# Attention output tiles moved from a stage of their own into the FFN blocks of a transformer layer, with smaller edge blocks and fewer small instructions

## The chip, the cores and the metric

The kernel runs on one core of a Trainium2 chip. The metric is device time in microseconds (us): the median of several executions. The profile is of one execution; its span is some 1 to 2 us shorter than the time. Engines: PE = TensorE, PEld = its weight loads, DVE = VectorE, ACT = ScalarE, POOL = GpSimd, SP = SyncE.

## The reference

One layer on 2048 tokens of width 576: layernorm with modulation, attention with a softmax feature map (32 heads of 18), output projection with a gate, layernorm again, an FFN of width 4608 with ReLU, and a second gate. Cut to what matters:

```python
pq = einsum('bhsd,hdf->bhsf', q, w_phi); pk = ...          # per head 18x18
phi_q = concat([softmax(pq), softmax(-pq)]); phi_k = ...
kv  = einsum('bhsf,bhsd->bhfd', phi_k, v);  z = phi_k.sum(over tokens)
num = einsum('bhqf,bhfd->bhqd', phi_q, kv)
o   = num / (einsum('bhqf,bhf->bhq', phi_q, z) + 1e-06)
x   = x + ga * (o @ wo)
h   = layernorm(x) * (1 + cb) + sb
x   = x + gb * (relu(h @ w1) @ w2)
```

`kv` sums over all tokens. So no token's attention output can begin before the whole K/V loop is through. After that point every tile of 128 tokens is independent.

## The kernel before

The program has a head (load, fold `w_phi` into Wk and Wq), a K/V loop over 16 token tiles, and then attention output and FFN. The parts that the change touches:

```python
def num_tile(t):                       # 128 tokens: 10 matmuls into three PSUM banks
    ...
    # eight small ACT copies bring the denominators from PSUM to dz
    # DVE: product, sum, reciprocal, product  (4 small instructions)
    # DVE: 4 multiplications PSUM x factor -> tmp
    nc.gpsimd.tensor_tensor(out=o_sb[:, t % NO, :], in0=tm[:, 0, :], in1=tm[:, 1, :], op=ALU.add)

def wo_tile(t):                        # 6 transposes of o_sb, ACT copy to oT, 10 matmuls with wo,
    ...                                # DVE adds the product to x_sb

def attn_out(b):                       # TPB = 4 tiles
    for t in range(b * TPB, (b + 1) * TPB):
        num_tile(t); wo_tile(t)
        ln_stats(1, t); ln_rstd(1, t, t + 1); ln_apply(1, t)
    ...
    to_features(b * TPB, TPB, ps1, h2T[b], 0, mod2, "vavav")     # transposes for the FFN

# ---- order of the program after the K/V loop
attn_out(0)
for b in range(1, NB): q_block(b, q_one)
...                                     # load of the last quarter of w2
for b in range(1, NB): attn_out(b)
for b in range(NB):    ffn1(b, ...); ffn2(b)
```

`ffn1` runs 18 pairs of hidden blocks (per pair eight 128-row and two 64-row matmuls of 512 columns). `ffn2` runs 36 matmuls of 288 columns for each half of each tile. The order on each engine is chosen by the compiler's scheduler from this program order. PE then ran its list in order: in the trace below it stands idle for one tile (1.20 us, to 235.53 us) although FFN matmuls follow in its list.

The softmax here doesn't subtract the row's maximum and nothing guards it: scores larger than these inputs give would overflow.

Of the kernel before, what the change touches and what calls it, by code (L numbers as in the profile page):

```python
# [8 lines left out]
P = 128  # L9
# [26 lines left out]
def kernel(  # L36
# [73 lines left out]
    NX = 4  # L110
    xn = small([P, NX, 640], BF16, "xn")
# [4 lines left out]
    dz = small([P, 2, 2, 2, 32], FP32, "dz")  # L116
    ab = small([P, 2, 5, 64], FP32, "ab")
# [19 lines left out]
    nc.sync.dma_start(x_sb[:, 1, :], xf[:, 1, :])  # L137
# [4 lines left out]
    nc.sync.dma_start(x_sb[:, 2:4, :], xf[:, 2:4, :])  # L142
    load_rows(nc.sync, wmod_sb[0], w_mod[:, 0:D], False)
    load_rows(nc.sync, wmod_sb[1], w_mod[:, D:2 * D], False)
    load_rows(nc.sync, wv_sb, A_wqkv[:, 2 * D:3 * D], True)
    nc.sync.dma_start(x_sb[:, 4:8, :], xf[:, 4:8, :])
    load_rows(nc.sync, wq_raw, A_wqkv[:, 0:D], False)
    nc.sync.dma_start(x_sb[:, 8:16, :], xf[:, 8:16, :])
    load_rows(nc.sync, wmod_sb[2], w_mod[:, 2 * D:3 * D], False)
    for i in (3, 4, 5):  # L150
        load_rows(nc.sync, wmod_sb[i], w_mod[:, i * D:(i + 1) * D], False)
    load_rows(nc.sync, wo_sb, A_wo, True)

    nc.vector.memset(eps_t[:], EPS)
    make_identity(nc, ident[:])
# [45 lines left out]

    def mod_row(i, dst):
        ps = two()
        for hf in range(2):
            for ck in range(NC):
                k = KR[ck]
                nc.tensor.matmul(ps[:, hf, 0:HD2], lhsT=rep[0:k, ck, :],
                                 rhs=wmod_sb[i][0:k, ck, hf * HD2:(hf + 1) * HD2],
                                 start=(ck == 0), stop=(ck == NC - 1))
        nc.scalar.activation(out=dst[:].rearrange("p (b f) -> p b f", b=2), in_=ps[:, :, 0:HD2], func=ACT.Copy)  # L210
# [9 lines left out]
    def fold_transposes(raw, dstT, engs):  # L220
        for g, (h0, nh) in enumerate(GRP):
            f0, nf = h0 * DH, nh * DH
            pt = one().bitcast(BF16)
# [36 lines left out]
    def ln_apply(n, t):  # L260
        y = xn[:, t % NX, :]
        for a, b, src in ((0, 576, 0), (576, 640, 512)):
            nc.vector.tensor_scalar(out=y[:, a:b], in0=x_sb[:, t, src:src + b - a],  # L263
                                    scalar1=rs[:, n, t, 0:1], scalar2=rs[:, n, t, 1:2],
                                    op0=ALU.mult, op1=ALU.add)

    def to_features(t0, nt, psum, dst, col0, mod, engs):
        for n, cs in enumerate(((0, 1), (2, 3), (4,))):
            pt = psum().bitcast(BF16).rearrange("p (c f) -> p c f", c=2)
            for k, ci in enumerate(cs):  # L270
                for j in range(nt):
                    nc.tensor.transpose(pt[:, k, j * P:(j + 1) * P],  # L272
                                        xn[:, (t0 + j) % NX, ci * P:(ci + 1) * P], ident[:, :])
            for k, ci in enumerate(cs):
                o_ = dst[:, ci, col0:col0 + nt * P]
                i_ = pt[:, k, 0:nt * P]
                if engs[ci] == "a":
                    nc.scalar.activation(out=o_, in_=i_, func=ACT.Identity,  # L278
                                         scale=mod[:, 1, ci:ci + 1], bias=mod[:, 0, ci:ci + 1])
                else:  # L280
                    nc.vector.tensor_scalar(out=o_, in0=i_, scalar1=mod[:, 1, ci:ci + 1],
                                            scalar2=mod[:, 0, ci:ci + 1], op0=ALU.mult, op1=ALU.add)
# [63 lines left out]
    def q_block(b, psum):  # L346
        sl = slice(b * TB, (b + 1) * TB)
        for gs in ((0, 1), (2, 3), (4,)):
            pss = psum(len(gs))
            for n, g in enumerate(gs):  # L350
                f0, nf = GRP[g][0] * DH, GRP[g][1] * DH
                for ci in range(4):
                    nc.tensor.matmul(pss[n][0:nf, :], lhsT=wq_sb[:, ci, f0:f0 + nf], rhs=hT[:, ci, sl],
                                     start=(ci == 0), stop=False)
            for n, g in enumerate(gs):
                f0, nf = GRP[g][0] * DH, GRP[g][1] * DH
                b0 = 64 * n
                nc.tensor.matmul(pss[n][0:nf, :], lhsT=wq_sb[b0:b0 + 64, 4, f0:f0 + nf],
                                 rhs=hT[b0:b0 + 64, 4, sl], start=False, stop=True)
            for n, g in enumerate(gs):  # L360
                nf = GRP[g][1] * DH
                for sgn in range(2):
                    nc.scalar.activation(out=Eq[b][0:nf, g, sgn, :], in_=pss[n][0:nf, :], func=ACT.Exp,
                                         scale=1.0 - 2.0 * sgn)
# [6 lines left out]
    fold_transposes(wk_raw, wkT, "a")  # L371
    for t in range(4):
        ln_stats(0, t)
        if t == 0:
            ln_rstd(0, 0, 1)
            ln_apply(0, 0)
    ln_rstd(0, 1, 4)
    for t in range(1, 4):
        ln_apply(0, t)
    mod_columns((0, 1), mod1)  # L380
    fold(wkT, wk_sb, "a")

    ENG_A = "avava"
    to_features(0, 4, one, hT, 0, mod1, "vvava")
    for t in range(NT + 2):
        if t < NT:
            if t % 4 == 0 and t + 4 < NT:
                for u in range(t + 4, t + 8):
                    ln_stats(0, u)
                ln_rstd(0, t + 4, t + 8)  # L390
            k_tile(t)
            v_tile(t)
        if 1 <= t <= NT:
            k_softmax(t - 1)
        if t >= 2:
            kv_tile(t - 2)
        if t < NT:
            if t + 4 < NT or t % 4 != 3:
                pass
            if t % 4 == 2 and t + 2 < NT:  # L400
                for u in range(t + 2, t + 6):
                    ln_apply(0, u)
                to_features(t + 2, 4, one, hT, (t + 2) * P, mod1, ENG_A)
        if t == 1:
            fold_transposes(wq_raw, wqT, "a")
        if t == 3:
            fold(wqT, wq_sb, "a")
        if t == 5:
            nc.gpsimd.tensor_copy(rep[:], siluc[:].unsqueeze(2).to_broadcast([P, NC, P]))
            mod_row(2, ga_row)  # L410
            for ci in range(NC):
                nc.gpsimd.tensor_tensor(out=wo_sb[:, ci, :], in0=wo_sb[:, ci, :], in1=ga_row[:], op=ALU.mult)
        if t == 7:
            mod_row(5, gb_row)
            mod_columns((3, 4), mod2)
        if t == 9:
            q_block(0, q_two)
    for g in range(NG):
        kv_final(g)
    actx.close()  # L420
# [13 lines left out]
    pa = ctx.enter_context(tc.tile_pool(name="pa", bufs=4, space=PS, reuse_waits="tile"))  # L434
    pf = ctx.enter_context(tc.tile_pool(name="pf", bufs=4, space=PS, reuse_waits="tile"))

    def ps1():
        return pa.tile([P, 512], FP32, name="psa")
# [7 lines left out]
    def num_tile(t):  # L446
        b, tok = t // TPB, slice((t % TPB) * P, (t % TPB + 1) * P)
        p0, p1_, p2_ = ps1(), ps1(), ps1()

        def mm(ps, col, g, sgn):  # L450
            nf, w = GRP[g][1] * DH, GRP[g][1] * (DH + 2)
            nc.tensor.matmul(ps[:, col:col + w], lhsT=Eq[b][0:nf, g, sgn, tok], rhs=kvzd[0:nf, g, sgn, 0:w],
                             start=True, stop=True)
        for g in range(3):
            mm(p0, g * 140, g, 0)
        for g in range(3):
            mm(p1_, g * 140, g, 1)
        for sgn in range(2):
            mm(p2_, sgn * 140, 3, sgn)
        for sgn in range(2):  # L460
            mm(p2_, 280 + sgn * 80, 4, sgn)
        d = dz[:, t % 2]
        for sgn, pp in ((0, p0), (1, p1_)):
            v = pp[:, 0:420].rearrange("p (g w) -> p g w", g=3)[:, :, 126:140]
            for k in range(2):
                nc.scalar.activation(out=d[:, k, sgn, 0:21].rearrange("p (g h) -> p g h", g=3),
                                     in_=v[:, :, 7 * k:7 * k + 7], func=ACT.Copy)
        v3 = p2_[:, 0:280].rearrange("p (s w) -> p s w", s=2)
        v4 = p2_[:, 280:440].rearrange("p (s w) -> p s w", s=2)
        for k in range(2):  # L470
            nc.scalar.activation(out=d[:, k, :, 21:28], in_=v3[:, :, 126 + 7 * k:133 + 7 * k], func=ACT.Copy)
            nc.scalar.activation(out=d[:, k, :, 28:32], in_=v4[:, :, 72 + 4 * k:76 + 4 * k], func=ACT.Copy)
        a = ab[:, t % 2].rearrange("p k (s h) -> p k s h", s=2)
        nc.vector.tensor_tensor(out=a[:, 0], in0=d[:, 0], in1=rev_pair(d[:, 1]), op=ALU.mult)
        nc.vector.tensor_tensor(out=a[:, 1, 0], in0=a[:, 0, 0], in1=a[:, 0, 1], op=ALU.add)
        nc.vector.reciprocal(out=a[:, 1, 1], in_=a[:, 1, 0])
        nc.vector.tensor_tensor(out=a[:, 2], in0=rev_pair(d[:, 1]),
                                in1=a[:, 1, 1].unsqueeze(1).to_broadcast([P, 2, H]), op=ALU.mult)
        A = a[:, 2]
        tm = tmp[:, t % NTMP]  # L480
        for sgn, pp in ((0, p0), (1, p1_)):
            nc.vector.tensor_tensor(  # L482
                out=tm[:, sgn, 0:378].rearrange("p (g h e) -> p g h e", g=3, e=DH),
                in0=pp[:, 0:420].rearrange("p (g w) -> p g w", g=3)[:, :, 0:126].rearrange("p g (h e) -> p g h e", e=DH),
# [112 lines left out]
```

## Time and profile before

511.6 us (median of 5; 510.88 to 512.5), span 509.8 us.

| Stage | us | what PE does |
|---|---|---|
| head | 0 to 25 | waits for loads and PSUM copies |
| K/V loop | 25 to 109 | almost full |
| opening: attention output before any FFN matmul | 109 to 156 | starves; from 136.7 us at half clock (0.50) |
| attention tiles mixed with FFN block 0 | 156 to 282 | waits about 1.2 us per tile |
| FFN blocks 1 to 3 alone | 282 to 505 | full |

From the page of the kernel before: the busy shares, then the 40 slices of the span. Each digit is a tenth; PEclk is the granted TensorE clock.

```profile
PE 460.6 (90%) x3259; PEld 275.7 (54%) x3278; DVE 227.0 (45%) x547; ACT 164.1 (32%) x433; POOL 59.6 (12%) x67
PE   1898899999648989898988999999999999999996
PEclk9999989999857999999999999999999999999999
```

PE is the engine that counts. Digits 6 and 4 in the eleventh and twelfth slice (127 to 153 us) and the 8, 5, 7 of the clock below them mark the opening. From 285 us to the last FFN matmul PE has no idle time left to gain: it is busy 219.96 of 220.60 us. In the head the clock row rests on no record: the first one is at 30.9 us. Four transposes take 0.69 us at 6.53 us, and 0.40 us at 235.53 us.

PE's waits of the kernel before in the window from 104 to 162 us, then from 162 to 285 us. The columns are: who waited, for whom, total us, times, longest.

```profile
PE psa L498 <- POOL o_sb L492: 10.9, 4, 5.6
...
PE psa L498 <- POOL o_sb L492: 13.1, 11, 1.5
```

L498 is the transpose of `o_sb`, the first PE work after the chain num, dz, DVE, POOL. It is by far the largest of PE's waits in these 180 us; the next are 1.9 us on `xn` and 1.6 us on `oT`. (Names such as rH, rV and rEQ in the lines are regions of memory that several tiles share.)

The timeline of PE in that opening (start, us, what, and in brackets the idle time before it and who ended it):

```profile
128.38 1.14 PE L287 MATMUL psa<-wo_sb,oT 128*128 128x288 bf16 x8
132.16 0.40 PE L358 MATMUL psf<-rH 64*72 64x512 bf16 x1
136.56 0.54 PE L498 MATMUL psa<-ident,o_sb 128*128 128x128 bf16 x4 [4.00 <-POOL o_sb L492]
138.14 2.10 PE L287 MATMUL psa<-wo_sb,oT 128*128 128x288 bf16 x8 [0.80 <-ACT oT L502]
147.39 0.61 PE L498 MATMUL psa<-ident,o_sb 128*128 128x128 bf16 x4 [5.61 <-POOL o_sb L492]
155.96 0.58 PE L526 MATMUL psf<-rHT,rW 128*128 128x512 bf16 x1
```

The last Q matmul ends at 132.6 us, and from there two tiles have nothing beside them. The eight matmuls of L287 take 2.10 us; in the first line, before the clock fell, they take 1.14 us. The clock records show half clock (0.50) from 136.7 us for 23.9 us.

A tile in the mixed stage of the kernel before:

```profile
228.83 0.54 PE L452 MATMUL psa<-kvzd,rEQ 126*128 126x140 bf16 x6
229.60 4.42 PEld L544 LDWEIGHTS <-rH 128*128 128x128 bf16 x37
234.08 1.39 POOL L492 TENSOR_TENSOR o_sb<-rV 128x576 bf16<-128x576 f32 x1 [8.00 <-PE psf L544]
235.53 0.40 PE L498 MATMUL psa<-ident,o_sb 128*128 128x128 bf16 x4 [1.20 <-POOL o_sb L492]
```

From num's first matmul to the end of the POOL sum it takes 235.47 - 228.83 = 6.64 us. The order on PE puts 37 FFN weights (and so 37 matmuls of 123 ns) after num before the transpose (34 to 39 for the tiles in this layer). PE stands 1.20 us.

### The profile page before, as it was taken

The page shows a single profiled execution, that of the slowest core. Times are in us where ns is not written, and L with a number is a line of the kernel's source. Part 1 is how long each engine was busy: PE and PEld are TensorE (multiplying, and loading weights), DVE is VectorE, ACT ScalarE, POOL GpSimd, SP SyncE. Part 2 cuts the span into 40 slices and gives each one's busy share as a digit, 9 for nine tenths or more (in the row PEclk, how much of TensorE's full clock was granted, in tenths as well). Part 3 has the DMA queues.
Part 4 walks back from the last instruction along what each step waited for, and adds up shares of the span by engine and source line. Part 5 has one row for each costly group of instructions (what it writes and reads, how often), then busy time and mean ns, then how long its engine had stood idle before and what let it go on. Part 6 is the DMA issues. An engine that isn't in the chain of part 4 may idle for free.

```text
span 509.8 us, 7862 instructions
## 1 busy us (share of the span) xinstructions
PE 460.6 (90%) x3259; PEld 275.7 (54%) x3278; DVE 227.0 (45%) x547; ACT 164.1 (32%) x433; POOL 59.6 (12%) x67
## 2 busy tenths in 40 slices
PE   1898899999648989898988999999999999999996
PEld 1766565654334434356665433677333777334775
DVE  5279972864344554446674533212333122333211
ACT  2467537757414545522312322000222000222000
POOL 4022632432111110211111000000000000000000
PEclk9999989999857999999999999999999999999999
DMA  8940038071030000000000000000000000000000
GB/s 247 347 127 2 1 111 308 2 244 71 1 104 0 1 1 2 1 0 13 13 2 12 13 0 1 1 23 13 13 0 3 12 13 13 11 1 0 13 13 24
DMA packets 17278, 22.64 MB, mean 44 GB/s; under 512 B 2010, under 2 KB 16602, under 8 KB 16730
## 3 DMA queue, kind: packets, MB, share of 16 engines
q1 hardware_dynamic: 16032, 22.12, 13.0%
q8 instruction: 25, 0.41, 0.3%
q10 hardware_dynamic: 1210, 0.02, 0.1%
q14 instruction: 11, 0.09, 0.0%
HBM read 19.78 MB, written 2.36 MB: 43 GB/s over the span
## 4 chain that ended last, share of the span: by engine, by line
PE 68%; DVE 19%; POOL 4%; ACT 4%; issue 2%; DMA 1%; POOLq 0%; DVEq 0%
PE psf L544 23%; PE psf L526 22%; POOL o_sb L492 4%; PE psf L530 4%; PE two L287 4%; PE psa L287 4%; DVE rV L482 3%; DVE st L251 2%; DVE xn L263 2%; DVE R_sb L316 2%; DVE rV L488 2%; DVE rH L320 2%; PE one L196 2%; DVE x_sb L506 1%; DMA x_sb<-in_A_x_dram 1%
## 5 line engine op out<-in xcount | busy, mean ns | idle before, releaser
L544 PEld LDWEIGHTS <-rH 128*128 128x128 bf16 x1152 | 111.4, 98 | 28.7 <-issue 0.9
L544 PE MATMUL psf<-rW,rH 128*128 128x288 bf16 x864 | 113.8, 286 | 0.0
L534 ACT ACTIVATE rH<-psf 128x512 bf16<-128x512 f32 x90 | 52.5, 597 | 164.6 <-PE psf L530 164.1
L526 PE MATMUL psf<-rEQ,rW 128*128 128x512 bf16 x420 | 101.8, 380 | 0.6
L526 PEld LDWEIGHTS <-rW 128*128 128x128 bf16 x576 | 50.8, 98 | 65.1 <-issue 16.7
L536 DVE TENSOR_SCALAR rH<-psf 128x512 bf16<-128x512 f32 x54 | 37.3, 692 | 76.2 <-PE psf L530 76.2
L547 DVE TENSOR_TENSOR yt<-psf,gb_row 128x288 f32<-128x288 f32 x32 | 14.6, 456 | 90.6 <-PE psf L544 90.5
L287 PE MATMUL two<-rW,rH 128*128 128x288 bf16 (+2 forms) x256 | 41.1, 300 | 0.5 <-ACT rH L278 0.2
L544 PE MATMUL psf<-rEQ,rH 128*128 128x288 bf16 x288 | 41.4, 286 | 0.0
L506 DVE TENSOR_TENSOR x_sb<-x_sb,psa 128x288 bf16<-128x288 bf16 x32 | 13.1, 451 | 62.5 <-PE psa L291 62.5
L492 POOL TENSOR_TENSOR o_sb<-rV 128x576 bf16<-128x576 f32 x16 | 22.4, 1403 | 147.1 <-DVE rV L488 130.6
L526 PE MATMUL psf<-rHT,rW 128*128 128x512 bf16 x137 | 36.9, 395 | 0.5 <-issue 0.4
L320 POOL TENSOR_TENSOR rH<-rH,R_sb 128x576 bf16<-128x576 bf16 x16 | 24.5, 1535 | 65.9 <-DVE R_sb L317 40.0
L498 PE MATMUL psa<-ident,o_sb 128*128 128x128 bf16 x64 | 6.7, 230 | 24.1 <-POOL o_sb L492 24.0
L287 PEld LDWEIGHTS <-rH 128*128 128x128 bf16 x256 | 23.4, 101 | 8.8 <-issue 0.8
L251 DVE BATCH_NORM_STATS2 st<-x_sb 128x6 f32<-128x288 bf16 x64 | 25.8, 438 | 3.6 <-DMA x_sb<-in_A_x_dram 3.6
L316 DVE TENSOR_REDUCE R_sb<-rH 128x64 f32<-128x1152 bf16 x16 | 21.5, 1342 | 12.9 <-ACT rH L302 12.8
L502 ACT ACTIVATE oT<-psa 128x640 bf16<-128x640 bf16 x16 | 11.2, 703 | 46.9 <-PE psa L500 46.8
L530 PEld LDWEIGHTS <-rW 64*128 64x128 bf16 x144 | 7.3, 93 | 29.7 <-issue 29.1
L302 ACT ACTIVATE rH<-two 128x576 bf16<-128x576 f32 x32 | 19.1, 649 | 13.4 <-PE two L291 9.7
L263 DVE TENSOR_SCALAR xn<-x_sb,rs 128x576 bf16<-128x576 bf16 x64 | 21.8, 383 | 0.6 <-PE one L272 0.4
L287 PE MATMUL psa<-wo_sb,oT 128*128 128x288 bf16 x128 | 20.3, 306 | 1.6 <-ACT oT L502 1.6
(93 smaller groups left out, 447.9 us busy)
## 6 DMA issues: line engine op xcount, KB each, us to landing
rW<-in_B_w_dram SPq DMA_DIRECT2D x1, 4608.0 KB
rW<-in_B_w_dram SPq DMA_DIRECT2D x3, 1296.0 KB, 9.5
rW<-in_w_mod_dram SPq DMA_DIRECT2D x6, 576.0 KB, 8.4
out_dram<-x_sb SPq DMA_DIRECT2D x16, 144.0 KB, 1.7
rW<-in_A_wqkv_dram SPq DMA_DIRECT2D x3, 576.0 KB, 6.2
rEQ<-in_B_w_dram SPq DMA_DIRECT2D x1, 1296.0 KB
x_sb<-in_A_x_dram SPq DMA_DIRECT2D x1, 1152.0 KB, 9.1
x_sb<-in_A_x_dram SPq DMA_DIRECT2D x1, 576.0 KB, 6.4
```

Source lines behind the costliest of these rows:

```text
L251: nc.vector.bn_stats(out=s[:, hf, :], in_=x_sb[:, t, hf * HD2:(hf + 1) * HD2])
L263: nc.vector.tensor_scalar(out=y[:, a:b], in0=x_sb[:, t, src:src + b - a], scalar1=rs[:, n, t, 0:1], scalar2=rs[:, n, t, 1:2], op0=ALU.mult ...
L287: nc.tensor.matmul(ps(bk)[:, 0:cn], lhsT=lhs(ci, 0, P), rhs=rhs[:, ci, c0:c0 + cn], start=(ci == 0), stop=False)
L302: nc.scalar.activation(out=E[:, sgn, :].rearrange("p (b f) -> p b f", b=2), in_=ps[:, :, 0:HD2], func=ACT.Exp, scale=1.0 - 2.0 * sgn)
L316: nc.vector.tensor_reduce(out=R[:, 0, :], in_=E, axis=AXX, op=ALU.add)
L320: eng.tensor_tensor(out=e, in0=e, in1=R[:, 1, sgn * H:(sgn + 1) * H].unsqueeze(2).to_broadcast([P, H, DH]), op=ALU.mult)
L492: nc.gpsimd.tensor_tensor(out=o_sb[:, t % NO, :], in0=tm[:, 0, :], in1=tm[:, 1, :], op=ALU.add)
L526: nc.tensor.matmul(hps[n][:], lhsT=w1a[:, ci, jj * P:(jj + 1) * P], rhs=h2T[b][:, ci, :], start=(ci == 0), stop=False)
L530: nc.tensor.matmul(hps[n][:], lhsT=w1b[b0:b0 + 64, j * P:(j + 1) * P], rhs=h2T[b][b0:b0 + 64, 4, :], start=False, stop=True)
L534: nc.scalar.activation(out=H1[:, jj, :], in_=hps[n][:], func=ACT.Relu)
L536: nc.vector.tensor_relu(H1[:, jj, :], hps[n][:])
L544: nc.tensor.matmul(ps[:, 0:cn], lhsT=H1[:, j, tt * P:(tt + 1) * P], rhs=w2q[j // 9][:, j % 9, c0:c0 + cn], start=(j == 0), stop=(j == NJ - 1))
```

## The change

The intent is to keep PE fed by other work while one tile's chain runs on ACT, DVE and POOL. Some words for what follows: *num* is the ten matmuls that begin a tile's chain, *dz* the denominators that ACT copies, `o_sb` the tile's attention output with which the chain ends, *oT* its transpose. A *Q group* is five matmuls with the exponentials of their result; there are 20. A *slot* is a place in an FFN block where other work may be laid: before each of the 18 pairs of `ffn1` and before each third (12 matmuls) of the 36 in `ffn2`. Only two tiles come before the first FFN block; the rest are laid between FFN matmuls of the block before the one that needs them. The diff, cut to its core (cuts marked `...`):

```diff
+    def a_filler(t):                       # inside the K/V loop
...
+        if 7 <= t < 14:
+            if t < 13:
+                q_part((t - 7) // 3, (t - 7) % 3, q_two)      # Q blocks 0 and 1
...
+    q_part(2, 0, q_two)
+    kv_tile(NT - 1)
     for g in range(NG):
         kv_final(g)
+    q_part(2, 2, q_two)
...
-        for sgn, pp in ((0, p0), (1, p1_)):        # dz: eight ACT copies -> three
...
+        nc.scalar.activation(out=d[:, :, 0:3]..., in_=ps[:, 0:2, 0:420]..., func=ACT.Copy)
...
+    FB = [(0, 2), (2, 4), (6, 4), (10, 4), (14, 2)]           # FFN blocks: first tile, tiles
+    ctx.enter_context(tc.manual_schedule(engines={mybir.EngineType.PE}))
+    num_tile(0)
+    q_part(2, 1, q_one)
+    q_part(3, 0, q_one)
+    num_tile(1)
+    tr_tile(0)
+    q_part(3, 1, q_one)
+    wo_tile(0)
+    q_part(3, 2, q_one)
+    tr_tile(1)
+    wo_tile(1)
+    for n in range(3):
+        feat(0, n)
+    for b in range(len(FB)):
...
+            last = 18 + 6 * FB[b][1]          # slots: 18 pairs, then thirds of 36 matmuls
+            step = 6 if b == 0 else 5
+            k0 = last - 4 - step * nt - 2
+            for i in range(nt):
...
+                put(k, num_tile, t)
+                put(k + step - 1, tr_tile, t)
+                put(k + step, wo_tile, t)
...
+        ffn(b, slots)
```

Besides: the layernorm output no longer carries a second copy of its last 64 columns (32 DVE instructions); 32 more transposes on PE make it. In the head, Wk's transposes use more PSUM banks, copies are shared between ACT and DVE, and the order of the first loads changes. The scaling of `wo` moves from POOL to DVE, and features are held in one buffer. Four parts of the change are not in the cut: num gets three PSUM banks and the transposes one of their own (before, both drew on a pool of four); the K/V loop does its layernorm tile by tile; it spreads the one-column matmuls of the second modulation, which the kernel before ran in one stretch; and half of the Relus of FFN block 0 go to DVE (before, all to ACT).

## The prediction

> **What bounds the kernel now.** TensorE (PE): the page gives it 460.6 of 509.8 us busy; next is DVE with 227. Four stages, from busy time by window and the timeline:
>
> - Head, 0 to 28 us: PE busy 8.4 of the first 20 us. Wk's transposes go through one PSUM bank, each waiting for its ACT copy (10.8, 12.5, 14.2, 16.0 us); K tile 0 starts near 25 us.
> - K/V loop, 28 to 104 us: PE busy 72.8 of 76 us.
> - Attention output mixed with Q and the first FFN block, 104 to 285 us. In 120:140 and 140:160 PE is busy 14.6 and 11.7 us, the clock 0.50 in the latter. PE's waits hold 24.0 us on the o_sb sum (POOL). [...]
> - Three FFN blocks alone, 285 to 506 us: 18 pairs of 2.15 us plus 35.4 us of second layer, 74.2 us each, no gaps.
>
> Matmuls at their undisturbed spacing (216 ns for 512 columns, 123 for 288, 57 for 128) make about 432 us of PE work. So 78 us is lost: head 18, K/V loop 8, 130 to 160 us 20, other mixed stretches 23, FFN 4, tail 5.
>
> **What the change does.** PE order is fixed by hand; attention tiles become fillers inside FFN blocks 0 to 3, so their DVE/ACT/POOL chains hide behind FFN matmuls ([...]in this trace DVE and ACT are mostly idle in the FFN). Eight more Q groups move into the K/V loop. FFN blocks become 2,4,4,4,2 tiles. Eight dz copies per tile become three; 32 DVE copies of 64 columns (320 ns) become 32 more PE transposes. The head gets more PSUM banks.
>
> **Cost.**
> - Head: 5 us earlier.
> - The cold stretch (20 us) goes.
> - Mixed losses (23 us, 1.7 us a tile): the num-to-o_sb chain takes 6.5 us (228.8 to 235.5 us); the gap given is 4 FFN2 slots (12 matmuls, 1.47 us each, so 5.9 us) or 5 FFN1 slots. I expect 0.5 to 1.5 us of wait per tile, 15 us in all with feature transposes.
> - New opening, two tiles with 7 Q groups (8 us) as cover before any FFN: 7 us lost.
> - Half-size FFN1 blocks: the two 64-row matmuls of a pair cost 0.42 us at 512 columns[...]: 36 pairs x 0.1 = 4 us. Extra transposes: 2.5 us.
> - DVE Relu queued behind the num chain, with four PSUM banks: 3 us.
>
> Span 510 - 5 - 20 - 23 + 15 + 7 + 6.5 + 3 - 3 (loop) = 490; the time is 1.8 us over the span. Since fillers may hide more, I put it at 488. All of this is on PE, hence on the critical path; the removed DVE and ACT instructions alone are worth nothing.
>
> **Predicted time** 488 us, 8 in 10 between 473 and 502. Faster by over 2%: 0.86; within 2%: 0.12; slower: 0.02.
>
> **Signs.** Right: no window at clock 0.50 after the head; FFN starts near 128 us; K tile 0 near 20 us; K/V loop ends near 108 us; PE's wait for o_sb under 12 us; a 256-column pair at 1.18 us. Wrong: PE waits on Relu above 8 us in block 0, or new clock drops.
>
> **What would make it wrong.** The opening starving long enough to drop the clock; DVE setting the pace in block 0 (about 8 of 10 us per tile); W1/W2 loads arriving after FFN wants them; or, on the good side, slots hiding the chain wholly (475).

510 - 5 - 20 - 23 + 15 + 7 + 6.5 + 3 - 3 is 490.5, where 6.5 is the 4 us and the 2.5 us of extra transposes. For starving and the clock, the trace of the kernel before shows PE idle for 4.00 us up to 136.56 us and the clock at 0.50 from 136.7 us.

## The result

The changed kernel takes 480.07 us (median of 9; 479.33 to 483.12) against 510.62 us (median of 16). The ratio is 0.941, 95% interval 0.939 to 0.943. Ratios here are the mean time of one kernel's runs over that of the other's of the same rounds, so not quite the ratio of the medians.

The page of the changed kernel, the same lines:

```profile
PE 456.9 (95%) x3478; PEld 287.8 (60%) x3490; DVE 236.4 (49%) x573; ACT 154.5 (32%) x359; POOL 53.8 (11%) x62
PE   3999999999699999999999999999999999999996
PEclk9999999999789999999999999999999999999999
```

One slice is still thin, the eleventh (120 to 132 us), and the clock still falls there once. PE's waits from 133.2 us to the end:

```profile
PE pt L523 <- POOL o_sb L517: 0.3, 1, 0.3
```

In the kernel before, 11 of the 12 tiles mixed with FFN block 0 waited, 13.1 us in all; in the changed kernel the 14 tiles that lie between FFN matmuls wait 0.3 us. A tile in FFN block 1 shows why:

```profile
229.78 0.74 PE L480 MATMUL num<-kvzd,rEQ 126*128 126x140 bf16 x10
230.32 5.77 PEld L580 LDWEIGHTS <-rH 128*128 128x128 bf16 x48
230.77 0.20 ACT L496 ACTIVATE dz<-num 128x16 f32<-128x16 f32 x1
231.35 0.22 DVE L500 TENSOR_TENSOR ab<-dz 128x70 f32<-128x70 f32 x1
234.68 1.40 POOL L517 TENSOR_TENSOR o_sb<-rV 128x576 bf16<-128x576 f32 x1 [9.80 <-DVE rV L513]
236.24 0.39 PE L523 MATMUL pt<-ident,o_sb 128*128 128x128 bf16 x4
```

The chain is hardly shorter: 236.08 - 229.78 = 6.30 us. But 48 matmuls now stand in front of the transpose instead of 37, and it follows 0.16 us after `o_sb` is written, with no idle time in brackets. Eight of the 14 tiles have 48 matmuls in the gap, the others 44 to 60 of several lengths. There is little to spare: on seven tiles the chain takes 6.6 to 6.8 us and the transpose starts 0.06 us after `o_sb`, the distance that it also has after each wait in the kernel before.

The opening of the changed kernel, the end of it:

```profile
124.04 0.40 PE L523 MATMUL pt<-ident,o_sb 128*128 128x128 bf16 x4 [0.88 <-POOL o_sb L517]
125.41 2.10 PE L306 MATMUL psf<-wo_sb,oT 128*128 128x288 bf16 x8 [0.80 <-ACT oT L526]
130.97 0.93 PE L289 MATMUL psf<-ident,xn 128*128 128x128 bf16 x7 [2.88 <-DVE xn L278]
133.23 1.91 PE L560 MATMUL psf<-h2T,rW 128*128 128x256 bf16 x8
```

Again three waits, and again the eight output matmuls at 2.10 us. The clock records of the trace hold 0.50 from 125.3 us for 10.2 us, against 23.9 us before.

By milestone (start times of PE's instructions in the two traces):

| Milestone, us | before | predicted | after |
|---|---|---|---|
| first matmul of K tile 0 | 25.0 | near 20 | 21.5 |
| last matmul of the K/V loop | 109.1 | 108 | 110.0 |
| first FFN matmul | 156.0 | 128 | 133.2 |
| last FFN matmul | 505.3 | | 474.4 |

The opening (last K/V matmul to first FFN matmul) shrank from 46.8 to 23.2 us, which is 23.6 us of the gain. From the first FFN matmul to the last it went from 349.3 to 341.1 us. That stretch is 8.2 us shorter although two more tiles lie in it (14, not 12) and the small blocks are dearer (1.20 us for a pair of 256 columns, against half of 2.15). The K/V loop ends at nearly the same time although five to six more Q groups of 1.1 us run before its last matmul (seven moved there, and the kernel before ran the start of Q block 1 there too). So some 6 us of what the opening lost is work moved ahead of it. The loop did get longer by it, 88.5 us instead of 84.1 from its first matmul to its last, but it starts 3.5 us sooner. It also no longer has the cold stretch (3.4 us at clock 0.50 from 71.8 us) that followed the one-column matmuls in the kernel before.

### The profile page after: what moved, and what is told of

It is laid out like the page before. It is cut to its first block, busy times and chain, and to the rows that moved or that the text cites. A ratio compares the mean times of both kernels' runs of the same rounds, so it can differ in the third digit from the quotient of the medians.

```text
span 479.0 us, 8186 instructions
## 1 busy us (share of the span) xinstructions
PE 456.9 (95%) x3478; PEld 287.8 (60%) x3490; DVE 236.4 (49%) x573; ACT 154.5 (32%) x359; POOL 53.8 (11%) x62
## 4 chain that ended last, share of the span: by engine, by line
PE 84%; DVE 9%; ACT 3%; DMA 1%; issue 1%; POOL 1%; POOLq 0%; SPq 0%; DVEq 0%
PE psf L580 29%; PE psf L560 28%; PE psf L564 5%; PE two L306 4%; PE psf L306 3%; PE num L480 2%; DVE st L268 2%; DVE R_sb L335 2%; PE two L372 2%; DMA x_sb<-in_A_x_dram 1%; DVE rH L339 1%; PE kvacc L348 1%; ACT rEQ L382 1%; PE pt L523 1%; ACT rH L321 1%
## 5 line engine op out<-in xcount | busy, mean ns | idle before, releaser
L560 PE MATMUL psf<-h2T,rW 128*128 128x512 bf16 (+1 forms) x708 | 140.8, 339 | 0.6
L570 DVE TENSOR_SCALAR rH<-psf 128x512 bf16<-128x512 f32 (+1 forms) x90 | 52.5, 584 | 93.9 <-PE psf L564 93.7
L560 PEld LDWEIGHTS <-rW 128*128 128x128 bf16 x720 | 63.9, 98 | 56.5 <-issue 11.3
L568 ACT ACTIVATE rH<-psf 128x512 bf16<-128x512 f32 (+1 forms) x90 | 46.0, 512 | 128.5 <-PE psf L564 128.5
L339 POOL TENSOR_TENSOR rH<-rH,R_sb 128x576 bf16<-128x576 bf16 x16 | 25.5, 1596 | 72.4 <-DVE R_sb L336 24.7
L564 PE MATMUL psf<-h2T,rW 64*128 64x512 bf16 (+1 forms) x180 | 31.4, 345 | 0.0
L526 ACT ACTIVATE oT<-pt 128x640 bf16<-128x640 bf16 x16 | 11.3, 708 | 52.0 <-PE pt L525 51.8
L533 DVE TENSOR_TENSOR x_sb<-x_sb,psf 128x288 bf16<-128x288 bf16 x32 | 13.1, 451 | 19.1 <-PE psf L310 19.1
L306 PE MATMUL psf<-wo_sb,oT 128*128 128x288 bf16 x128 | 19.3, 296 | 0.8 <-ACT oT L526 0.8
L272 ACT ACTIVATE rs<-mv,eps_t 128x1 f32<-128x1 f32 (+2 forms) x24 | 7.0, 300 | 32.5 <-DVE mv L269 32.5
L507 DVE TENSOR_TENSOR rV<-num,ab 128x378 f32<-128x378 f32 x32 | 16.1, 545 | 1.3 <-PE psf L564 0.5
```

The costliest lines, as they stand in the source:

```text
L306: nc.tensor.matmul(ps(bk)[:, 0:cn], lhsT=lhs(ci, 0, P), rhs=rhs[:, ci, c0:c0 + cn], start=(ci == 0), stop=False)
L339: eng.tensor_tensor(out=e, in0=e, in1=R[:, 1, sgn * H:(sgn + 1) * H].unsqueeze(2).to_broadcast([P, H, DH]), op=ALU.mult)
L507: nc.vector.tensor_tensor(out=tm[:, sgn, 0:378].rearrange("p (g h e) -> p g h e", g=3, e=DH), in0=ps[:, sgn, 0:420].rearrange("p (g w) -> ...
L560: nc.tensor.matmul(hps[n][:, 0:nn], lhsT=w1a[:, ci, jj * P:(jj + 1) * P], rhs=h2T[:, ci, 0:nn], start=(ci == 0), stop=False)
L564: nc.tensor.matmul(hps[n][:, 0:nn], lhsT=w1b[b0:b0 + 64, j * P:(j + 1) * P], rhs=h2T[b0:b0 + 64, 4, 0:nn], start=False, stop=True)
L568: nc.scalar.activation(out=H1[:, jj, 0:nn], in_=hps[n][:, 0:nn], func=ACT.Relu)
```

## The experiments

Theory A: PE executes its list in order, and the gain comes from how much other PE work stands between a tile's num and its transpose: mostly 48 matmuls in the FFN, and two tiles instead of four in the opening. Rivals: the fixed hand order itself; the cheaper small instructions; the head.

All runs gave correct results, and all had 3 rounds or, in the last group, 5. Kernels named together ran on the same chip beside the same runs of the kernel before.

### First group

**auto.** The hand order is taken away.

```diff
-    ctx.enter_context(tc.manual_schedule(engines={mybir.EngineType.PE}))
```

> The changed kernel without the one line that fixes TensorE's order by hand; all else as changed. Theory (the hand order holds the gain of the mixed stage: TensorE executes in order, and a transpose of o_sb put too early stalls it): waits for o_sb come back, some 0.7 to 1.5 us for each of 14 tiles, 490 to 505 us. Rival (the slots in program order are enough, any scheduler keeps them): 478 to 483 us, with waits for o_sb near the 1.2 us of the changed kernel.

Measured: 480.65 us, ratio 0.944 (0.940 to 0.947), the same as the change. The compiler's order did differ (in the opening, the second output product stood elsewhere), but PE's waits for `o_sb` stayed at 1.5 us in all:

```profile
PE pt L523 <- POOL o_sb L517: 1.5, 2, 0.9
```

My version of theory A, that fixing the order by hand was needed, fell. Where the slots stand in the program was enough here: the scheduler kept them.

**four_open.** Blocks of four tiles, so four tiles come before the FFN.

```diff
-    FB = [(0, 2), (2, 4), (6, 4), (10, 4), (14, 2)]
+    FB = [(0, 4), (4, 4), (8, 4), (12, 4)]
...
     tr_tile(1)
+    num_tile(2)
     wo_tile(1)
+    tr_tile(2)
+    num_tile(3)
+    load_w2q3()
+    wo_tile(2)
+    tr_tile(3)
+    wo_tile(3)
```

> The changed kernel with FFN blocks of 4,4,4,4 tiles in place of 2,4,4,4,2, so four tiles of attention output come before the first FFN matmul. Theory (the starved opening is what the small first block pays for): the opening grows by two tiles of about 9 us with 3 us of TensorE work each, at half clock for most of it, so +12 to +16 us, less 4 us for the 256-column pairs saved: 488 to 493 us, and a stretch at clock 0.50 of 20 us or more in place of 10 us. Rival (the half blocks cost as much as they save): 480 us or less.

Measured: 486.14 us, ratio 0.954 (0.950 to 0.957), 6 us worse than the change, a little less than expected. The first FFN matmul comes at 149.0 us, 15.7 us later. The clock records hold 0.50 for 20.5 us. From there to the end it takes 336 us against 345.8, which fits two tiles fewer and no half blocks in it. PE's longest wait of that run:

```profile
PE pt L523 <- POOL o_sb L517: 8.4, 3, 4.5
```

The small first block pays here: it costs less than the starving that it saves (but see four_fill).

**tr_early.** Each transpose one slot earlier.

```diff
-                put(k + step - 1, tr_tile, t)
+                put(k + step - 2, tr_tile, t)
```

> The changed kernel with each o transpose one slot earlier (12 second-layer matmuls, 1.47 us, or one first-layer pair). Theory (in the changed kernel the chain from num to o_sb ends about 0.1 us before TensorE reaches the transpose, so there is no reserve): each of 14 tiles waits 1.0 to 1.4 us more, waits for o_sb 14 to 20 us in total, 494 to 500 us. Rival (the slots have reserve and the order itself is what counts): under 483 us.

Measured: 496.75 us, ratio 0.974 (0.971 to 0.977): 16 us lost by moving 14 groups of six transposes by one slot. PE's waits from 133 us on:

```profile
PE pt L523 <- POOL o_sb L517: 14.2, 11, 1.7
```

About 1.3 us each time, and nearly all of the 14.4 us by which the profiled spans differ. The three tiles that do not wait have 48 second-layer matmuls in the gap, or some of the longer first-layer ones. This is also about the wait of the kernel before, which had 37 matmuls in the gap where this run, in the second FFN layer, has 36. Since everything else of the change is in this run, theory A stands for the mixed stage, with the number: 48 matmuls hide the chain, 36 do not.

**before_cheap.** The kernel before with cheaper small instructions alone.

```diff
-            for k in range(2):
-                nc.scalar.activation(out=d[:, k, sgn, 0:21]..., in_=v[:, :, 7 * k:7 * k + 7], func=ACT.Copy)
+            nc.scalar.activation(out=d[:, :, sgn, 0:21]..., in_=v..., func=ACT.Copy)     # 8 copies -> 4
...
-        for a, b, src in ((0, 576, 0), (576, 640, 512)):
+        nc.vector.tensor_scalar(out=y[:, 0:576], ...)       # no second copy; 32 more transposes
```

> The kernel before with only the cheaper instructions: four dz copies for eight, and the 64-column DVE copies of xn replaced by 32 more TensorE transposes; order and blocks as before. Theory on record (the removed DVE and ACT instructions alone are worth nothing): ratio to before 0.995 to 1.006. Rival (they shorten the num-to-o_sb chain that TensorE waits for at 15 tiles, by about 0.3 us of ACT and 0.3 us of DVE each): 502 to 506 us, ratio 0.98 to 0.99.

Measured: 511.77 us, ratio 1.004 (1.001 to 1.008). Nothing gained, as the prediction said, and PE still waits 23.0 us for `o_sb` (24.0 us before):

```profile
PE psa L502 <- POOL o_sb L496: 23.0, 16, 5.5
```

The run added 32 transposes to PE, some 1.8 us at the 56 to 57 ns of these traces, so a gain of up to about that size could hide behind them; the 3 us or more of the rival could not.

### Second group

**control.** The changed kernel again.

```diff
+# the changed kernel again, as a control
```

> The changed kernel again, with a comment added, as the control for the three runs beside it: 479 to 482 us, ratio to before near 0.941.

Measured: 481.82 us, ratio 0.945 (0.942 to 0.948). Its four executions fall in two pairs: 480.6 and 481.1 us at a mean granted clock of 0.987, and 482.5 and 482.6 us at 0.984. The profiled one, of the second pair, has a second cold stretch of 3.4 us, at 32.1 us in the K/V loop. So whether the clock drops seems to differ from one execution to the next of the same kernel, and goes with over 1 us (482.5 against 481.1).

**fill.** Three Q groups from the K/V loop into the opening.

```diff
-            if t < 13:
+            if t < 11:
                 q_part((t - 7) // 3, (t - 7) % 3, q_two)
...
     q_part(3, 2, q_one)
+    q_part(1, 2, q_one)
     tr_tile(1)
     wo_tile(1)
+    q_part(1, 1, q_one)
```

> The changed kernel with three Q groups (q_part(1,1) and q_part(1,2)) taken out of the K/V loop and put into the opening, before the second o transpose and before the feature transposes, where TensorE waits 0.9 + 0.8 + 2.9 us and then runs 10 us at clock 0.50. Theory (the opening has idle TensorE time and a cold clock for want of work, and the K/V loop is full): the loop ends 3 us earlier, the first FFN matmul starts 4 to 6 us earlier, no or a shorter cold stretch: 473 to 477 us. Rival (the opening is paced by the chain of the two tiles on ACT and DVE, and three more Q groups with six more exponentials on ACT lengthen it as much): 479 to 482 us.

Measured: 477.65 us, ratio 0.938 (0.935 to 0.941), 4.2 us better than the control by the medians. That is just above the range of the theory (473 to 477), with a control that was itself 1.7 us above the changed kernel's first median. Without the control's two slower executions, and without the one of fill at clock 0.995 (the others have 0.998 and 0.999), some 3.5 us remain. The end of the opening:

```profile
124.02 1.16 PE L306 MATMUL psf<-wo_sb,oT 128*128 128x288 bf16 x8 [1.34 <-ACT oT L526]
128.51 0.56 PE L289 MATMUL psf<-ident,xn 128*128 128x128 bf16 x7 [0.71 <-DVE xn L278]
131.56 1.05 PE L560 MATMUL psf<-h2T,rW 128*128 128x256 bf16 x8
132.76 1.05 PE L560 MATMUL psf<-h2T,rW 128*128 128x256 bf16 x8
```

The waits shrink, and the same eight output matmuls take 1.16 us instead of 2.10: the clock never drops between 25.5 us and 472.6 us, and the first FFN matmul comes at 129.8 us. How much of the gain is idle time filled and how much is the clock, this run doesn't separate. The work was the same and was only moved to where PE had stood idle.

**old_head.** The changed kernel with the old head.

```diff
-            if g == 4:
+            if g == 4 or single:               # Wk: one PSUM bank, copies all on ACT
...
-    fold_transposes(wk_raw, wkT, "aav")
+    fold_transposes(wk_raw, wkT, "a", True)
...
-    fold(wkT, wk_sb, "ava")
     mod_columns((0, 1), mod1)
+    fold(wkT, wk_sb, "a")
```

> The changed kernel with the head of the kernel before: Wk transposes through one PSUM bank with all copies on ACT, the modulation columns before the fold, the old order of the first loads. Prediction on record: 5 us worth, so 485 us. What the trace of the changed kernel suggests (K tile 0's first matmul at 21.5 us in place of 25.0, but undisturbed streaming only from 25.3 in place of 27.1): 2 to 4 us, 482 to 484 us.

Measured: 482.61 us, ratio 0.947 (0.945 to 0.950), against 0.945 for the control: about 1 us, with overlapping intervals. K tile 0 begins at 25.65 us instead of 21.39 (4.3 us later), but the last K/V matmul is only 2.2 us later and the first FFN matmul 1.6 us later. Most of the gain of the head is given back on the way. A likely reason is DVE, which is full there. Busy time of the changed kernel from 30 to 50 us:

```profile
30.00:50.00 20.00, 18.79 (x182) 12.61 (x180) 20.00 (x47) 16.35 (x41) 5.88 (x4) 1.00 0.02 4
```

The third number after the span is DVE: 20.00 of 20 us. Starting K tiles sooner may only meet a full DVE sooner. This reason is read from the profile; no run took DVE work out of that stretch, so it is argued, not shown.

**dz8.** The changed kernel with the old eight dz copies.

```diff
-        nc.scalar.activation(out=d[:, :, 0:3]..., in_=ps[:, 0:2, 0:420]..., func=ACT.Copy)
-        ... (3 in all)
+        for sgn in range(2):
+            v = ps[:, sgn, 0:420].rearrange("p (g w) -> p g w", g=3)[:, :, 126:140]
+            for k in range(2):
+                nc.scalar.activation(out=d[:, sgn, 0:3, k, :], in_=v[:, :, 7 * k:7 * k + 7], func=ACT.Copy)
+        ... (8 in all)
```

> The changed kernel with the eight small ACT copies of dz of the kernel before in place of three. Theory (no reserve between the end of the chain and the transpose, as the one-slot-earlier run showed): the chain gets 0.3 to 0.4 us longer, 14 tiles wait 0.2 to 0.35 us each, 483 to 485 us. In the kernel before, the same cheapening was worth nothing. Rival (worth nothing here either): within 1.5 us of the control.

Measured: 481.90 us, ratio 0.945 (0.943 to 0.948), the same as the control. My theory that the chain would grow fell for the tiles between FFN matmuls. The same tile in that run:

```profile
231.36 0.74 PE L480 MATMUL num<-kvzd,rEQ 126*128 126x140 bf16 x10
232.20 0.81 DVE L268 BATCH_NORM_STATS2 st<-x_sb 128x6 f32<-128x288 bf16 x2
232.61 0.25 ACT L498 ACTIVATE dz<-num 128x8 f32<-128x8 f32 x1
232.93 0.21 DVE L501 TENSOR_TENSOR ab<-dz 128x70 f32<-128x70 f32 x1
236.25 1.40 POOL L518 TENSOR_TENSOR o_sb<-rV 128x576 bf16<-128x576 f32 x1 [9.48 <-DVE rV L514]
```

From num to POOL it takes 236.25 - 231.36 = 4.89 us; in the changed kernel 234.68 - 229.78 = 4.90 us. The last dz copy ends 1.50 us after num's start instead of 1.19, yet DVE begins the chain 1.57 us after num's start in both, because it is busy with the previous tile's residual and layernorm until then. The copies had 0.38 us of slack, and the five extra ones used about 0.31 us of it. In the opening, where DVE had no such work, the chains did grow, from 5.6 to 5.9 and from 6.9 to 7.6 us, and PE waited 1.8 us for `o_sb` instead of 1.1; the time doesn't show it.

### Third group

**fill_again.** The control of this group, `fill` with a comment added.

```diff
+# the version with three Q groups in the opening again
```

> The version with three Q groups moved into the opening, again, as the control for the three beside it: 476.5 to 478.6 us.

Measured: 477.14 us, ratio 0.935 (0.933 to 0.937).

**fill5.** Two more Q groups moved.

```diff
-            if t < 11:
+            if t < 10:
...
     tr_tile(1)
+    q_part(1, 0, q_one)
     wo_tile(1)
```

> Two more Q groups (all five of Q block 1) moved from the K/V loop into the opening, between the second o transpose and its output product, where TensorE still waits 1.3 us for the ACT copy oT. Theory (TensorE's idle time is what pays): 2.2 us leave the loop, about 1.3 us of them fall into the wait, and the rest delays the feature chain: 1 to 1.5 us better than fill_again, 475.5 to 477 us. Rival (ACT, with four more exponentials in the opening, delays oT and the layernorm): the same or up to 2 us worse.

Measured: 475.72 us, ratio 0.933 (0.931 to 0.935), 1.4 us better than fill_again by the medians; the intervals of the ratios overlap, but the four times of each (475.3 to 476.7 and 477.0 to 477.4) do not. The 1.3 us wait for oT is gone from PE's list. It is the fastest of all by its median. Against the changed kernel it wins by 0.933 to 0.941 or 0.945, about 1%.

**four_fill.** Four tiles first, twelve Q groups between their steps. The last line of the cut sums up the order of the calls.

```diff
-    FB = [(0, 2), (2, 4), (6, 4), (10, 4), (14, 2)]
+    FB = [(0, 4), (4, 4), (8, 4), (12, 4)]
...
+    # num0 q21 q30 num1 tr0 q31 wo0 q32 num2 tr1 q10 wo1 num3 tr2 q11 wo2 q12 tr3 wo3
```

> Four tiles ahead of the first FFN block as in the four-tile run (486 us), but with twelve Q groups laid between their steps, five of them taken out of the K/V loop. Theory (the four-tile opening lost by lack of cover and by clock, not by its length): the loop ends 5 us earlier, the first FFN matmul starts near 138 us in place of 149, the cold stretch is 10 us or less, the whole 474 to 479 us, about equal to fill_again, since 4 us of 256-column overhead are saved and about as much is lost at the end of the opening. Rival (the opening is paced by the tiles' own chain on DVE, some 9 us a tile): 481 us or more.

Measured: 477.09 us, ratio 0.935 (0.932 to 0.937). With cover, the opening of four tiles loses only 1.1 us to `o_sb` instead of 8.4, and the first FFN matmul comes at 140.0 us instead of 149.0. The size of the first block hardly matters once the opening has work; the missing work was the cost. Here the clock may still drop: the profiled execution, with 6.8 us at 0.50, took 478.2 us, the two with a mean clock of 0.996 took 476.0 and 476.5.

**step6.** In FFN blocks 1 to 3, tiles six slots apart instead of five.

```diff
-            step = 6 if b == 0 else 5
+            step = 6
```

> As fill_again, with tiles six slots apart instead of five in FFN blocks 1 to 3, so each o transpose comes 1.47 us after its o_sb is ready. Theory (at five slots the chain is just hidden, more distance buys nothing, while one slot less cost 16 us): within 1 us of fill_again, waits for o_sb as there. Rival (small waits of other kinds, for PSUM or oT, still hide in the five-slot spacing): 1.5 to 3 us better.

Measured: 476.49 us, ratio 0.934 (0.932 to 0.936), 0.65 us better than fill_again and within its interval. One slot less cost 16 us, one slot more brings too little to tell from noise: the spacing of the change is at the knee.

## Why the prediction was right or wrong

The predicted time (488, range 473 to 502) held and the direction was right. The sum was about 11 us high in span (490 against 479). Point by point:

- "PE is the bound, and all that counts is on PE": right. before_cheap and dz8 changed only DVE and ACT instructions (before_cheap added transposes, too) and moved nothing that the noise lets one see.
- "PE order is fixed by hand": right as a description, but it is not what matters. auto shows the same time without it.
- "The cold stretch (20 us) goes" and "new opening ... 7 us lost": these two terms were taken apart wrongly. The clock still drops for 10.2 us, and the first FFN matmul comes at 133.2 us instead of 128. I had named this as a way to be wrong. fill shows what it is worth: some 3.5 to 4 us, for three Q groups.
- "Mixed losses: 0.5 to 1.5 us of wait per tile, 15 us in all": this is the mis-sized term that mattered. The waits for `o_sb` measured 0.3 us after the opening. I set a chain of 6.5 us, counted from num's first matmul, against four slots of 1.47 us, counted from num's last. Num's own ten matmuls (0.54 us until the FFN weights begin) belong in the gap: 0.54 + 5.9 = 6.4 us, against a chain of 6.3. tr_early shows the size of what was at stake: 16 us.
- "Head: 5 us": mis-sized. K tile 0 is 3.5 us earlier, the time about 1 us (old_head). I took a stage's head start for its worth, without asking what the next stage would meet.
- "Half-size FFN1 blocks 4 us, a 256-column pair at 1.18 us": right. A pair takes 132.76 - 131.56 = 1.20 us in the opening lines of fill, against half of 2.15; 36 pairs make 4.5 us. The two 64-row matmuls take 0.42 us of a pair at 512 columns and 0.31 us at 256 (from the starts of PE's matmuls in the traces: 312 and 319 ns before and after them, less the 216 ns of a full matmul; 205 and 212 ns, less 109). No run tests why.
- "DVE Relu queued behind the num chain, 3 us": wrong. PE has no wait on a Relu in the whole mixed stage, so DVE's Relus never set the pace in block 0.
- "K/V loop ends near 108 us": nearly right, 110.0 us, though not by the head start that I counted on.

How the errors add up: the first FFN matmul came 5 us later than predicted (head and opening together), and the stretch from there to the end of the span took 345.8 us instead of the 362 that the sum implied, about 16 us less. The two terms that did not show up in it, 15 us of waits and 3 us of Relu, account for that within 2 us.

## What to carry to other kernels

When one tile's work passes through several engines, count from the trace how much independent work the bottleneck engine (here PE, which ran its list in order) has between sending that tile off and needing it back, in the same endpoints for both; then place the return just after the chain ends: here one slot less cost 16 us, half of what the whole change gained, and one slot more cost nothing. Work that is the same wherever it stands should be moved to where the bottleneck engine idles, at stage openings above all, even out of a stage that is full (fill: 4.2 us by the medians, the clock's share not separated). Shortening an instruction of a chain did not pay where another queue held the next link back (dz8), and a stage that started 4.3 us sooner gained about 1 us in the end (old_head).
